# A list schedule that treats the SBUF port of VectorE and GpSimd as one resource, and an activation that stays in its PSUM bank

## The chip, the cores and the metric

The kernel runs on one core of one Trainium2 chip. The metric is the device time of one execution, in microseconds, lower is better; it is a little longer than the span from the first to the last instruction that the profiler records.

## The reference

Three layers follow each other: a linear attention with RMS norm, a block with a squared ReLU, and a block with SiLU. Matrices are float32 and are multiplied to nearly float32 accuracy.

```
# attention: 8 batches x 8 heads, 576 tokens, head size 64
kv = einsum('bhsd,bhse->bhde', k, v); out = einsum('bhsd,bhde->bhse', q, kv)
x  = out / sqrt(mean(out*out, -1) + 1e-6) * g_norm          # -> 4608 x 512
# first block: w_in 512 x 2048, w_out 2048 x 512
h = x @ w_in; r = maximum(h, 0); y = (s * (r*r) + b) @ w_out
# second block, the same sizes
h = y @ w_in2; out = (h / (1 + exp(-h))) @ w_out2
```

## The kernel before, in words

Every float32 operand of a product is split into a high part (rounded by ScalarE, `rnd`, L201) and a low part (the difference, `rest`, L204), and three matmuls (high x high, high x low, low x high) make one product. The 4608 tokens are nine blocks of 512. The weights come as 64-bit numbers and are decoded on the chip: ScalarE takes the magnitude (`mag`, L284) and the low word (`carry`, L301), VectorE the sign bit and the exponent (`sign`, L288; `top`, L293), GpSimd adds the two words (`total`, L307), then ScalarE and VectorE split the result (L201, L204).

The first block runs plainly for token blocks 0 to 6, one unit for each of the 16 slices of 128 hidden features: 12 matmuls into one of two PSUM banks `h` (`mm1`), ReLU out of the bank into an SBUF tile `g` (`first`, L722), the square (`squares`: on GpSimd in token block 0, L728, on ScalarE in the others, L726), scale and bias (`affine`, L731), the split of `g` into `gh` (L201 and L204), and 12 matmuls into four accumulators (`mm2`). There are two tiles `g`. In token block 0 the weights are being decoded while the units run; that stretch reaches from about 31 to 162 us. Attention of the later token blocks and a recoding of all weights for the next stage run beside blocks 1 to 6.

The other blocks (7 and 8 in the first layer, all but block 6 in the second) go through in pairs by a Strassen scheme with seven products instead of eight (L931 for the hidden layer, L1059 to L1061 for the output). VectorE takes sums out of PSUM (`plus`, L956; `total`, L1068); the differences of the activations (`minus`, L995) and the low parts (L204) may go to VectorE or GpSimd, the sums of results (L1093, L1110) go to GpSimd. Block 6 of the second layer is again plain and ends the program.

The order on each engine is not written by hand. `Plan` (its `run`) is a list scheduler: each operation has a key, the engines that may do it with a planned duration for each, what it needs and makes, and the buffers it takes and gives back. At every step the scheduler takes, of the engines' ready operations, the one that can begin first. It writes one in-order program for each engine; on the chip an instruction that waits holds up all behind it on its engine. `both` and `both2` give the planned durations of an operation that VectorE or GpSimd may do.

Of the kernel before, what the change touches and what calls it, by code (L numbers as in the profile page):

```python
# [12 lines left out]
ALU = mybir.AluOpType  # L13


class Plan:
# [24 lines left out]
    def run(self):  # L41
# [3 lines left out]
        dma = 0.0  # L45
# [71 lines left out]
def kernel(  # L117
# [25 lines left out]
    P = 128  # L143
# [68 lines left out]
    def dma(dst, src):  # L212
# [46 lines left out]
    def decode(layer, kind, m, c, width, sfx, key, needs=(), quarter=None, made=()):  # L259
# [63 lines left out]
        add({DVE: 0.07 + width * 0.52e-3}, key - 0.45, sign, needs=[f(1)], makes=[f(2)])  # L323
        add(dve(width), key - 0.4, top, needs=[f(2)], makes=[f(3)])
        add(act(width) if layer == 0 else {DVE: 0.07 + width * 0.52e-3}, key - 0.35, carry, needs=[f(0)], makes=[f(4)])
        add({POOL: 0.19 + width * 2.46e-3}, key - 0.25, total, needs=[f(3), f(4)], makes=[f(6)] + list(made), gives=[raw])
        w = f"w{kind}{m}"
        if layer == 0:
# [4 lines left out]
            add(dve(width), key - 0.15, lo, needs=[f(7)], makes=[full], gives=[dw])  # L333
# [87 lines left out]
    def attention_pair(bb, p, key, before=None):  # L421
# [110 lines left out]
        add({DVE: 0.2}, key + 0.5, lambda e: rest(e, st["kvl"], st["kvf"], st["kvh"]), needs=[f("kvh")], makes=[f("kvl")],  # L532
# [91 lines left out]
    g_t, h_t, a_t, xs = {}, {}, {}, {}  # L624
# [57 lines left out]
    def unit(u):  # L682
# [605 lines left out]
```

## Time and profile before

| what | value |
|---|---|
| median of 3 runs | 1610.23 us (1607.92 to 1613.66) |
| the profiled execution, its own time | 1611.14 us |
| its span, first to last instruction | 1609.4 us |
| mean granted TensorE clock | 0.996 |
| busy: PE, VectorE, ScalarE, GpSimd | 1576.7, 1072.7, 903.4, 1031.6 us |

The profile is of one execution. The busy time of PE is a union of overlapping matmuls, so a busy PE may still start fewer matmuls than it could. The busy time of VectorE and GpSimd holds the time in which an instruction has started and stands still.

### The profile page before, as it was taken

Reading aid. Unit: us, or ns where it says so; the run is one execution under the profiler, and the core shown is the slowest. Engines: PE = TensorE matmul, PEld = TensorE weight load, DVE = VectorE, ACT = ScalarE, POOL = GpSimd, SP = SyncE. Lnnn points to the kernel's source line nnn. Section 1 sums busy time; section 2 is a strip of 40 time slices with the busy share of each in tenths; the row PEclk is TensorE's granted clock in tenths of the full one; section 3 lists DMA queues with packets and bytes.
Section 4 is the critical chain, followed back from the end, with each engine's and each line's share of the span. In section 5 each row is a group of like instructions: output and inputs, shape, how many; then the busy total and the mean of one; then the engine's idle time right before and its main releaser. Section 6 shows DMA issues by size and latency. Waiting matters only on the chain.

```text
span 1609.4 us, 23497 instructions
## 1 busy us (share of the span) xinstructions
PE 1576.7 (98%) x7473; PEld 1279.5 (80%) x7473; DVE 1072.7 (67%) x1526; ACT 903.4 (56%) x1700; POOL 1031.6 (64%) x865
## 2 busy tenths in 40 slices
PE   8889999999999999999999999999999999999999
PEld 6667888878877787777888878888888888888887
DVE  5997667677677877552767876786688558856510
ACT  5787656666666766765766453544354435444222
POOL 4775777655556665565557796777678667866632
PEclk9999999999999999999999999999999999999999
DMA  9755678666667786799567786878687868776684
GB/s 222 186 165 134 219 232 249 206 189 188 189 202 220 217 243 189 235 335 314 182 193 226 250 292 187 259 222 241 192 286 197 233 196 265 196 239 193 204 212 134
DMA packets 377147, 351.30 MB, mean 218 GB/s; under 512 B 178240, under 2 KB 288832, under 8 KB 377024
## 3 DMA queue, kind: packets, MB, share of 16 engines
q1 hardware_dynamic: 376896, 349.81, 72.8%
q8 instruction: 59, 0.97, 0.3%
q14 instruction: 64, 0.52, 0.1%
q0 software_dynamic: 128, 0.00, 0.0%
HBM read 254.28 MB, written 95.42 MB: 217 GB/s over the span
## 4 chain that ended last, share of the span: by engine, by line
PE 81%; DMA 8%; DVE 6%; issue 2%; SPq 1%; ACT 1%; POOL 1%; DVEq 0%; POOLq 0%; ACTq 0%
PE hp L931 23%; PE acc L1059 8%; PE acc L1061 8%; PE acc L1060 8%; PE h L198 5%; PE h L196 5%; PE h L197 5%; PE acc L196 4%; PE acc L197 4%; PE acc L198 4%; DMA xt_d<-tmp 2%; SPq L213 1%; DVE raw L288 1%; PE kv_ps L481 1%; DVE raw L293 1%
## 5 line engine op out<-in xcount | busy, mean ns | idle before, releaser
L931 PE MATMUL hp<-xo,win 128*128 128x512 f32 x1680 | 424.4, 390 | 5.0 <-DVE tmp L956 5.0
L931 PEld LDWEIGHTS hp<-xo,win 128*128 128x128 f32 x1680 | 315.0, 188 | 74.9 <-DVE tmp L956 7.3
L204 POOL TENSOR_TENSOR g<-tmp,g 128x512 fp32r<-128x512 f32 x167 | 237.4, 1429 | 175.8 <-ACT g L201 174.8
L1068 DVE TENSOR_TENSOR ya<-acc,ya 128x512 f32<-128x512 f32 x210 | 142.8, 684 | 120.8 <-PE acc L1061 120.3
L1059 PE MATMUL acc<-g,wout 128*128 128x512 f32 x560 | 219.6, 392 | 0.1
L1061 PE MATMUL acc<-g,wout 128*128 128x512 f32 x560 | 218.9, 391 | 0.0
L1060 PE MATMUL acc<-g,wout 128*128 128x512 f32 x560 | 218.9, 391 | 0.0
L201 ACT ACTIVATE g<-tmp 128x512 fp32r<-128x512 f32 x280 | 172.7, 629 | 81.1 <-POOL tmp L995 34.5
L722 ACT ACTIVATE g<-h 128x512 f32<-128x512 f32 x128 | 76.2, 595 | 209.8 <-PE h L198 205.7
L198 PE MATMUL h<-xh,wi 128*128 128x512 f32 x448 | 177.1, 395 | 9.5 <-DVE wi L204 9.4
L196 PE MATMUL acc<-gh,wo 128*128 128x512 f32 x448 | 182.5, 407 | 1.7 <-DVE y L210 0.9
L196 PE MATMUL h<-xh,wi 128*128 128x512 f32 x448 | 177.8, 397 | 0.3 <-ACT wi L201 0.3
L197 PE MATMUL acc<-gh,wo 128*128 128x512 f32 x448 | 176.1, 393 | 1.6 <-POOL gh L204 1.6
L197 PE MATMUL h<-xl,wi 128*128 128x512 f32 x448 | 176.4, 394 | 0.3 <-POOL xl L204 0.3
L198 PE MATMUL acc<-gh,wo 128*128 128x512 f32 x448 | 175.5, 392 | 0.0
L956 DVE TENSOR_TENSOR tmp<-hp,tmp 128x512 f32<-128x512 f32 x200 | 136.7, 685 | 53.9 <-PE hp L931 50.6
L204 DVE TENSOR_TENSOR g<-tmp,g 128x512 fp32r<-128x512 f32 x113 | 150.9, 1354 | 19.5 <-ACT g L201 18.8
L995 POOL TENSOR_TENSOR tmp<-tmp 128x512 f32<-128x512 f32 x85 | 133.5, 1577 | 28.5 <-ACT tmp L977 14.0
L977 ACT ACTIVATE tmp<-tmp 128x512 f32<-128x512 f32 x120 | 75.5, 629 | 125.7 <-DVE tmp L956 125.1
L204 POOL TENSOR_TENSOR gh<-g,gh 128x512 fp32r<-128x512 f32 x70 | 97.7, 1397 | 60.6 <-ACT gh L201 50.8
L1059 PEld LDWEIGHTS acc<-g,wout 128*128 128x128 f32 x560 | 105.1, 188 | 23.4 <-DVE ya L1068 0.9
L1061 PEld LDWEIGHTS acc<-g,wout 128*128 128x128 f32 x560 | 105.2, 188 | 23.3
(142 smaller groups left out, 2963.3 us busy)
## 6 DMA issues: line engine op xcount, KB each, us to landing
wout<-wo SPq DMA_DIRECT2D x312, 256.0 KB, 3.9
win<-wi SPq DMA_DIRECT2D x120, 512.0 KB, 4.8
wi<-rq SPq DMA_DIRECT2D x192, 128.0 KB, 2.5
wo<-rq SPq DMA_DIRECT2D x192, 128.0 KB, 2.4
win<-wi SPq DMA_DIRECT2D x72, 256.0 KB, 3.9
raw<-in_moe_w_out_dram SPq DMA_DIRECT2D x38, 256.0 KB, 3.5
raw<-in_moe_w_in_dram SPq DMA_DIRECT2D x34, 256.0 KB, 3.0
xt_d<-tmp SPq DMA_DIRECT2D x32, 256.0 KB, 5.7
```

The source lines that it names most:

```text
L196: nc.tensor.matmul(ps, wh, xh, start=first, stop=False)
L197: nc.tensor.matmul(ps, wh, xl, start=False, stop=False)
L198: nc.tensor.matmul(ps, wl, xh, start=False, stop=last)
L201: nc.scalar.activation(hi, src, AF.Copy)
L204: eng[e].tensor_tensor(lo, src, f32(hi), op=ALU.subtract)
L931: nc.tensor.matmul(ps, w[:, wn, f_], x_[:, xn], start=first and n == 0, stop=kk == KH - 1 and n == 2, skip_group_check=True)
L956: nc.vector.tensor_tensor(t, bank[me, a], tmp[b_, me], op=ALU.add)
L995: eng[e].tensor_tensor(t, tmp[a, me], tmp[b_, me], op=ALU.subtract)
L1059: nc.tensor.matmul(ps, w[:, 0, dd], gh, start=a == 0, stop=False)
L1060: nc.tensor.matmul(ps, w[:, 0, dd], gl, start=False, stop=False)
L1061: nc.tensor.matmul(ps, w[:, 1, dd], gh, start=False, stop=a == 1)
L1068: nc.vector.tensor_tensor(y2[tp, i, d], st["ps"], y2[tp, i, d], op=ALU.add)
```

## The change

The scheduler gets a fifth kind of resource. A duration of the class `Port` marks an operation that uses the SBUF port which VectorE and GpSimd share; such an operation begins, in the plan, only after the last one so marked has ended, on whichever of the two engines. The planned durations of these operations become shorter (those of an instruction alone). An operation that two engines may do is no longer a candidate on an engine if the other would end it sooner (`best_on`). And in the plain units `g` is no longer a tile in SBUF: ReLU, square and affine work in place in the PSUM bank `h`, the split reads the bank, and the bank is given back only after the low part is taken. The square of token block 0 moves from GpSimd to ScalarE, the low part of all plain units goes to VectorE alone, and the two tiles `g0`, `g1` go to the pool `ya` of the Strassen sums from the start.

```diff
+class Port(float):
+    pass
...
         def begin(e, op, when):
-            t = max(free[e], when)
+            t = max(free[e], when, port if isinstance(op[2][e], Port) else 0.0)
...
+        def best_on(e, t, op, ready):
+            if len(op[2]) == 1:
+                return True
+            for e2, d2 in op[2].items():
+                if e2 != e:
+                    t2 = begin(e2, op, ready[e2][op[1]][1])
+                    if t2 is not None and (t2 + d2, e2) < (t + op[2][e], e):
+                        return False
+            return True
...
-                cand = [(t, op) for t, op in cand if t is not None]
+                cand = [(t, op) for t, op in cand if t is not None and best_on(e, t, op, ready)]
...
                 free[e] = end = t + op[2][e]
+                if isinstance(op[2][e], Port):
+                    port = end
...
-                 "g": ["g0", "g1"], "gh": ["gh0", "gh1", "gh2"], "y": ["y0", "y1"],
+                 "gh": ["gh0", "gh1", "gh2"], "y": ["y0", "y1"],
...
     def both(n):
-
-        return {DVE: 0.1 + n * 1.8e-3, POOL: 0.15 + n * 2.4e-3}
-
-    def both2(n):
-        return {DVE: 0.15 + n * 2.25e-3, POOL: 0.15 + n * 2.65e-3}
+        return {DVE: Port(0.07 + n * 1.05e-3), POOL: Port(0.15 + n * 2.36e-3)}
...
-        add({POOL: 0.19 + width * 2.46e-3}, key - 0.25, total, needs=[f(3), f(4)], makes=[f(6)] + list(made), gives=[raw])
+        add({POOL: Port(0.27 + width * 1.67e-3)}, key - 0.25, total, needs=[f(3), f(4)], makes=[f(6)] + list(made), gives=[raw])
...
-            nc.scalar.activation(g_t[u], h_t[u], AF.Relu if layer == 0 else AF.Silu)
+            nc.scalar.activation(h_t[u], h_t[u], AF.Relu if layer == 0 else AF.Silu)
...
-        add(act(T), u + 0.1, first, needs=[("mm1", u, KD - 1)], makes=[("r", u)], takes=[g], gives=[("h", u)])
+        add(act(T), u + 0.1, first, needs=[("mm1", u, KD - 1)], makes=[("r", u)])
         src = ("r", u)
         if layer == 0:
-            add({POOL: 1.1} if t == 0 else act2(T), u + 0.2, squares, needs=[src], makes=[("sq", u)])
-            add({ACT: 0.81}, u + 0.25, affine, needs=[("sq", u)], makes=[("aff", u)])
+            add(act(T), u + 0.2, squares, needs=[src], makes=[("sq", u)])
+            add({ACT: 0.73}, u + 0.25, affine, needs=[("sq", u)], makes=[("aff", u)])
...
-        add({POOL: 1.4} if layer == 0 and t == 0 else both(T), u + 0.35, g_lo, needs=[("gh", u)], makes=[("gl", u)], gives=[g])
+        add({DVE: 0.69}, u + 0.35, g_lo, needs=[("gh", u)], makes=[("gl", u)], gives=[("h", u)])
```

In the whole program GpSimd goes from 870 to 273 instructions and VectorE from 1528 to 2094. ScalarE gets 16 squares more.

GpSimd in token block 0 (`dw<-raw` is `total` of a weight, `g<-g` the square, `gh<-g,gh` the low part of a unit), before:

```order
L307 TENSOR_TENSOR dw_942<-raw_902 128x512
L204 TENSOR_TENSOR gh_976<-g_936,gh_975 128x512
L307 TENSOR_TENSOR dw_987<-raw_932 128x512
L728 TENSOR_TENSOR g_1014<-g_1014 128x512
L307 TENSOR_TENSOR dw_1008<-raw_949 128x512
L307 TENSOR_TENSOR dw_1023<-raw_978 128x512
L204 TENSOR_TENSOR gh_1058<-g_1014,gh_1057 128x512
L728 TENSOR_TENSOR g_1068<-g_1068 128x512
```

and now:

```order
L319 TENSOR_TENSOR dw_918<-raw_835 128x512
L319 TENSOR_TENSOR dw_927<-raw_863 128x512
L319 TENSOR_TENSOR dw_946<-raw_898 128x512
L319 TENSOR_TENSOR dw_1000<-raw_959 128x512
L319 TENSOR_TENSOR dw_1040<-raw_982 128x512
```

Only the sums of the weights are left on GpSimd there. VectorE at the same place, around the low parts of weights `wo6` and `wi8`, before:

```order
L204 TENSOR_TENSOR wi7_1036<-dw_987,wi7_1036 128x512
L288 TENSOR_SCALAR raw_994<-raw_994 128x512
L293 SCALAR_TENSOR_TENSOR raw_994<-dw_1042,raw_994 128x512
L578 RECIPROCAL rms_1073<-rms_1073 128x16
L583 STREAM_TRANSPOSE sq_969<-rms_1073 128x512
L204 TENSOR_TENSOR wo6_1075<-dw_1008,wo6_1075 128x512
L590 SCALAR_TENSOR_TENSOR x32_802<-o_ps_944,vecs_121,sq_969 128x512
L204 TENSOR_TENSOR wi8_1085<-dw_1023,wi8_1085 128x512
```

and now:

```order
L220 TENSOR_TENSOR gh_1029<-h_939,gh_1028 128x512
L305 SCALAR_TENSOR_TENSOR raw_959<-dw_1000,raw_959 128x512
L300 TENSOR_SCALAR raw_982<-raw_982 128x512
L220 TENSOR_TENSOR wi7_1061<-dw_946,wi7_1061 128x512
L590 RECIPROCAL rms_1071<-rms_1071 128x16
L305 SCALAR_TENSOR_TENSOR raw_982<-dw_1040,raw_982 128x512
L595 STREAM_TRANSPOSE sq_1009<-rms_1071 128x512
L220 TENSOR_TENSOR gh_1093<-h_1004,gh_1092 128x512
L220 TENSOR_TENSOR wo6_1089<-dw_1000,wo6_1089 128x512
L602 SCALAR_TENSOR_TENSOR x32_891<-o_ps_990,vecs_121,sq_1009 128x512
L220 TENSOR_TENSOR wi8_1117<-dw_1040,wi8_1117 128x512
```

The same operations stand there with one low part of a unit (`gh<-h,gh`) more per unit, read from the PSUM bank. PE before the first output matmuls of unit 0 (`h_760` is the bank of unit 3, all 24 matmuls of units 2 and 3 stand ahead of the output; `acc<-gh,wo0` is the output of unit 0), before:

```order
L196 MATMUL h_760<-xh_645,wi3_728 128x512
L197 MATMUL h_760<-xl_646,wi3_728 128x512
L198 MATMUL h_760<-xh_645,wi3_728 128x512
L508 MATMUL r_ps_792<-qT_708,kvf1_131 128x64
L196 MATMUL acc_796<-gh_757,wo0_583 128x512
L197 MATMUL acc_796<-gh_758,wo0_583 128x512
L198 MATMUL acc_796<-gh_757,wo0_583 128x512
```

and now, after 33 short filler matmuls (`warm`; `h_767` is the bank of unit 2):

```order
L1231 MATMUL warm_146<-zeros_119 128x256
L212 MATMUL acc_758<-gh_731,wo0_616 128x512
L213 MATMUL acc_758<-gh_732,wo0_616 128x512
L214 MATMUL acc_758<-gh_731,wo0_616 128x512
L212 MATMUL h_767<-xh_359,wi2_675 128x512
L213 MATMUL h_767<-xl_360,wi2_675 128x512
L214 MATMUL h_767<-xh_359,wi2_675 128x512
L212 MATMUL acc_776<-gh_731,wo0_616 128x512
```

Units 2 and 3 of the hidden layer have moved behind the first output of unit 0, whose bank unit 2 needs. VectorE in the Strassen stage, around one group of activations (`g2` are the low parts, `hp` and `acc` PSUM banks), before:

```order
L995 TENSOR_TENSOR tmp_11808<-tmp_11691,tmp_11689 128x512
L995 TENSOR_TENSOR tmp_11822<-tmp_11735,tmp_11808 128x512
L204 TENSOR_TENSOR g2_11829<-tmp_11808,g2_11828 128x512
L204 TENSOR_TENSOR g2_11841<-tmp_11822,g2_11841 128x512
L956 TENSOR_TENSOR tmp_11864<-hp_11795,tmp_11799 128x512
```

and now:

```order
L997 TENSOR_TENSOR tmp_11713<-tmp_11548,tmp_11602 128x512
L220 TENSOR_TENSOR g2_11707<-tmp_11687,g2_11707 128x512
L997 TENSOR_TENSOR tmp_11548<-tmp_11634,tmp_11548 128x512
L997 TENSOR_TENSOR tmp_11733<-tmp_11634,tmp_11713 128x512
L220 TENSOR_TENSOR g2_11726<-tmp_11713,g2_11725 128x512
L220 TENSOR_TENSOR g2_11738<-tmp_11548,g2_11738 128x512
L997 TENSOR_TENSOR tmp_11687<-tmp_11687,tmp_11733 128x512
L220 TENSOR_TENSOR g2_11745<-tmp_11733,g2_11745 128x512
L958 TENSOR_TENSOR tmp_11772<-hp_11709,tmp_11715 128x512
```

The differences and low parts that GpSimd took stand in VectorE's own queue, eight ahead of the next sum out of a PSUM bank instead of four.

## Rows read from the trace of the kernel before

**Rows 1.** Windows; columns: length, PE, PEld, DVE, ACT, POOL busy, clock, DMA, GB/s.
```profile
31.00:162.00 131.00, 118.28 (x619) 91.36 (x618) 118.04 (x160) 101.11 (x200) 90.03 (x74) 0.96 0.63 169
162.00:640.00 478.00, 473.20 (x2431) 382.98 (x2431) 342.43 (x608) 318.28 (x676) 294.60 (x328) 1.00 0.71 212
640.00:800.00 160.00, 154.09 (x670) 124.60 (x668) 80.90 (x93) 106.47 (x182) 93.45 (x71) 1.00 0.82 268
800.00:1560.00 760.00, 759.21 (x3322) 623.05 (x3321) 517.13 (x640) 351.86 (x590) 530.99 (x367) 1.00 0.75 225
```
**Rows 2.** Waits of PE, 31 to 162 us: total, times, longest.
```profile
PE h L198 <- DVE wi L204: 9.4, 7, 3.1
```
**Rows 3.** Timeline of PE: start, duration; units 0 and 16 begin here.
```profile
30.93 0.48 PE L196 MATMUL h<-xh,wi 128*128 128x512 f32 x1
...
151.06 0.40 PE L198 MATMUL h<-xh,wi 128*128 128x512 f32 x1
151.29 0.39 PE L196 MATMUL h<-xh,wi 128*128 128x512 f32 x1
```
**Rows 4.** Groups of VectorE by form, 31 to 162 us.
```profile
L293 DVE SCALAR_TENSOR_TENSOR raw<-dw,raw 128x512 uint32<-128x512 uint32 x26 | 29.1, 1121 | 0.5
L288 DVE TENSOR_SCALAR raw<-raw 128x512 uint32<-128x512 uint32 x26 | 23.8, 920 | 1.9 <-ACT dw L284 1.9
L204 DVE TENSOR_TENSOR wi<-dw,wi 128x512 fp32r<-128x512 f32 x15 | 15.7, 1045 | 0.0
L204 DVE TENSOR_TENSOR wo<-dw,wo 128x512 fp32r<-128x512 f32 x13 | 12.2, 935 | 2.3 <-ACT wo L201 2.3
```
**Rows 5.** Timeline of VectorE, 82 to 91 us.
```profile
82.30 1.26 DVE L288 TENSOR_SCALAR raw<-raw 128x512 uint32<-128x512 uint32 x1
...
90.10 0.68 DVE L293 SCALAR_TENSOR_TENSOR raw<-dw,raw 128x512 uint32<-128x512 uint32 x1
90.71 0.41 DVE L288 TENSOR_SCALAR raw<-raw 128x512 uint32<-128x512 uint32 x1
```
**Rows 6.** Timeline of GpSimd, 82 to 100 us.
```profile
82.00 1.27 POOL L307 TENSOR_TENSOR dw<-raw 128x512 uint32<-128x512 uint32 x1 [0.78 <-ACT gh L201]
...
98.72 1.04 POOL L307 TENSOR_TENSOR dw<-raw 128x512 uint32<-128x512 uint32 x1 [0.68 <-ACT raw L301]
```
**Rows 7.** Groups of GpSimd by form, 31 to 162 us.
```profile
L307 POOL TENSOR_TENSOR dw<-raw 128x512 uint32<-128x512 uint32 x27 | 33.8, 1252 | 22.1 <-ACT dw L284 5.2 <-DVE raw L293 4.3 <-ACT raw L301 3.3
L204 POOL TENSOR_TENSOR gh<-g,gh 128x512 fp32r<-128x512 f32 x16 | 24.6, 1546 | 4.5 <-ACT gh L201 4.5
```
**Rows 8.** Tile g, 36 to 53 us: ns least, median, most; first to last start.
```profile
L722 ACT ACTIVATE g<-h x3: 584/597/601, 43.9 to 52.6; 128x512 f32<-128x512 f32 x3
L731 ACT ACTIVATE g<-g,vecs x2: 799/800/800, 48.4 to 49.9; 128x512 f32<-128x512 f32 x2
L201 ACT ACTIVATE gh<-g x2: 616/617/618, 49.3 to 50.7; 128x512 fp32r<-128x512 f32 x2
L204 POOL TENSOR_TENSOR gh<-g,gh x2: 1717/1732/1746, 50.9 to 52.6; 128x512 fp32r<-128x512 f32 x2
```
**Rows 9.** Timeline of PE, 56 to 57.3 us: first output matmul of unit 0.
```profile
56.88 0.77 PE L196 MATMUL acc<-gh,wo 128*128 128x512 f32 x1
```
**Rows 10.** Waits of PE, 640 to 1560 us.
```profile
PE hp L931 <- DVE tmp L956: 5.0, 4, 2.7
```
**Rows 11.** Groups of VectorE by form, 800 to 1560 us.
```profile
L204 DVE TENSOR_TENSOR g<-tmp,g 128x512 fp32r<-128x512 f32 x106 | 140.4, 1344 | 18.6 <-ACT g L201 17.9
L956 DVE TENSOR_TENSOR tmp<-hp,tmp 128x512 f32<-128x512 f32 x184 | 125.8, 685 | 41.1 <-PE hp L931 39.9
L995 DVE TENSOR_TENSOR tmp<-tmp 128x512 f32<-128x512 f32 x69 | 77.3, 1125 | 12.9 <-POOL tmp L995 8.3 <-ACT tmp L977 2.7 <-ACT tmp L983 1.1
```
**Rows 12.** Groups of GpSimd by form, 800 to 1560 us.
```profile
L204 POOL TENSOR_TENSOR g<-tmp,g 128x512 fp32r<-128x512 f32 x155 | 219.7, 1424 | 161.2 <-ACT g L201 160.2 <-POOL tmp L995 0.9
L1093 POOL TENSOR_TENSOR ya<-ya 128x512 f32<-128x512 f32 x70 | 99.3, 1449 | 12.7 <-DVE ya L1068 12.5
```

More of the change, by code (lines that the diff above doesn't have):

```diff
@@ L44, in run @@
         free["PE"] = self.PE_START
-        dma = 0.0
+        dma = port = 0.0
         known, waiting, left = {}, {}, {}
@@ L322, in decode @@
             makes=[f(1)], takes=[dw])
-        add({DVE: 0.07 + width * 0.52e-3}, key - 0.45, sign, needs=[f(1)], makes=[f(2)])
-        add(dve(width), key - 0.4, top, needs=[f(2)], makes=[f(3)])
-        add(act(width) if layer == 0 else {DVE: 0.07 + width * 0.52e-3}, key - 0.35, carry, needs=[f(0)], makes=[f(4)])
-        add({POOL: 0.19 + width * 2.46e-3}, key - 0.25, total, needs=[f(3), f(4)], makes=[f(6)] + list(made), gives=[raw])
+        add({DVE: Port(0.07 + width * 0.62e-3)}, key - 0.45, sign, needs=[f(1)], makes=[f(2)])
+        add({DVE: both(width)[DVE]}, key - 0.4, top, needs=[f(2)], makes=[f(3)])
+        add(act(width) if layer == 0 else {DVE: Port(0.07 + width * 0.62e-3)}, key - 0.35, carry, needs=[f(0)], makes=[f(4)])
+        add({POOL: Port(0.27 + width * 1.67e-3)}, key - 0.25, total, needs=[f(3), f(4)], makes=[f(6)] + list(made), gives=[raw])
         w = f"w{kind}{m}"
@@ L332, in decode @@
                 takes=takes)
-            add(dve(width), key - 0.15, lo, needs=[f(7)], makes=[full], gives=[dw])
+            add({DVE: both(width)[DVE]}, key - 0.15, lo, needs=[f(7)], makes=[full], gives=[dw])
     def rq(b):
@@ L531, in attention_pair @@
         add({ACT: 0.2}, key + 0.4, kv_hi, needs=[f("kvf")], makes=[f("kvh")], takes=[b["kvs"]], gives=[b["kvf"]])
-        add({DVE: 0.2}, key + 0.5, lambda e: rest(e, st["kvl"], st["kvf"], st["kvh"]), needs=[f("kvh")], makes=[f("kvl")],
+        add({DVE: Port(0.2)}, key + 0.5, lambda e: rest(e, st["kvl"], st["kvf"], st["kvh"]), needs=[f("kvh")], makes=[f("kvl")],
             gives=[b["kvf"]])
@@ L897, in pair_x @@
         add(act2(T), k2, hi, needs=[("xl2",) + me], makes=[("pxh",) + me], takes=[b_], gives=[rb])
-        add(both2(T), k2 + 0.02, lo, needs=[("pxh",) + me], makes=[("xo", i, tp, kk)], gives=[rb])
+        add(both(T), k2 + 0.02, lo, needs=[("pxh",) + me], makes=[("xo", i, tp, kk)], gives=[rb])
     def win_loads(tp, j):
@@ L999, in hidden @@
         kt = k(6) + 0.2
[L1000 to L1003 removed]
+        add(both(T), kt, minus("e", "a", "d"), needs=sg("a", "d"), makes=sg("e"), takes=[tb["e"]])
+        add(both(T), kt + 0.02, minus("f", "b", "e"), needs=sg("b", "e"), makes=sg("f"), takes=[tb["f"]])
+        add(both(T), kt + 0.01, minus("a", "b", "a"), needs=sg("b", "e"), makes=sg("a2"))
+        add(both(T), kt + 0.1, minus("c", "c", "f"), needs=sg("f") + [("gl",) + me + (B21,)], makes=sg("c2"))
         for i, src, ready, kk, gives in (
@@ L1018, in hidden @@
             add(act2(T), kk, hi, needs=ready, makes=[("gh",) + me + (i,)], takes=[gb])
-            add(both2(T), kk + 0.03, lo, needs=[("gh",) + me + (i,)], makes=[("gl",) + me + (i,)],
+            add(both(T), kk + 0.03, lo, needs=[("gh",) + me + (i,)], makes=[("gl",) + me + (i,)],
                 gives={B11: [], B22: [], B21: [], T1: [tb["e"]], T3: [tb["a"]], T2: [], T4: [tb["c"]]}[i])
@@ L1093, in go @@
                     eng[e].tensor_tensor(y2[tp, i, d], y2[tp, i, d], y2[tp, j, d], op=ALU.add)
-                add({POOL: 1.3}, key + 0.02 * n, go, needs=needs + ([o(0)] if n == 1 else []), makes=[o(n)], gives=[y(x) for x in gives])
+                add({POOL: Port(1.36)}, key + 0.02 * n, go, needs=needs + ([o(0)] if n == 1 else []), makes=[o(n)], gives=[y(x) for x in gives])
             parts = ((0, 0, B21, 1), (0, 1, B22, 4), (1, 1, T1, 5), (1, 0, T4, 6))
@@ L1110, in go @@
                         eng[e].tensor_tensor(y2[tp, dst, d], y2[tp, a, d], y2[tp, b_, d], op=ALU.subtract)
-                    add({POOL: 1.3}, key + 0.3 + 0.02 * m, go, needs=needs, makes=[("xs0", tp, so, d)])
+                    add({POOL: Port(1.36)}, key + 0.3 + 0.02 * m, go, needs=needs, makes=[("xs0", tp, so, d)])
                     after = {T1: [("xs0", tp, T2, d)], T2: [("xs0", tp, T4, d)]}.get(so, [])
```

26 lines of the change are left out of this document (6 added, 20 removed).

## The prediction

> **What bounds the kernel now.** I read the busy times by stretch first. From 162 to 640 us PE is busy for 473.2 of 478 us, from 800 to 1560 us for 759.2 of 760 [rows 1]. There PE is the bound, the change takes no matmul of the product away, and nothing is to be won. What can be won lies in two stretches: token block 0 with the decoding of the weights (31 to 162 us, PE busy 118.3 of 131) and the passage into the Strassen stage (640 to 800 us, 154.1 of 160) [rows 1].
>
> In the first of them the waits of PE name one cause, the low part of a decoded weight from VectorE, 9.4 us of visible idleness [rows 2]. The visible idleness is not all of the loss. Matmuls that follow each other start 0.23 us apart [rows 3], so the 24 matmuls of a unit need 24 x 0.23 = 5.5 us; unit 0 begins at 30.93 and unit 16 at 151.29 us [rows 3], which is 7.5 us per unit. Sixteen units lose 32 us, of which the attention matmuls that share the stretch take a part. The granted clock has a mean of 0.96 there, against 1.00 in the stretches that PE fills [rows 1].
>
> VectorE is busy for 118.0 of these 131 us, ScalarE for 101.1, GpSimd for 90.0 [rows 1]. But VectorE does not work all that time. The sign of a half weight takes 0.41 us alone and 0.92 in the mean; `top` 0.68 alone and 1.12 in the mean; the low parts, with two SBUF inputs of the same size, 1.05 and 0.94 [rows 4, 5]. The slow ones lie over GpSimd's instructions: the sign that starts at 82.30 takes 1.26 us beside a sum that runs from 82.00 to 83.27 [rows 5, 6]. So VectorE stands behind GpSimd, and PE behind VectorE.
>
> **The lock, part by part.** The lost time of VectorE in the stretch is 26 x (0.92 - 0.41) + 26 x (1.12 - 0.68) + 15 x (1.045 - 0.68) + 13 x (0.935 - 0.68) = 13.3 + 11.4 + 5.5 + 3.3 = 33.5 us [rows 4, 5]. What holds it up are GpSimd's 90 us [rows 1]. The squares and the low parts of the units leave GpSimd, as do three `xl` and one `qTl`; what stays are 27 sums of 1.04 us alone, 28 us [rows 6, 7], and, in the order of instructions, eight half as wide, at half of that 4 us (an estimate). That is 32 of 90. If the loss goes with GpSimd's time, 33.5 x 32/90 = 12 us are left and 21.5 saved.
>
> VectorE also gets work: 16 low parts read from PSUM and about four instructions of the same size. Alone and back to back they start about 0.61 us apart [rows 5]: 20 x 0.61 = 12 us. A VectorE difference with a PSUM input is no dearer than 0.685 us in the Strassen stage [rows 11], the price of one alone. Net VectorE has 118 - 21.5 + 12 = 108.5 us to do; at the same filling (118 of 131) the stretch takes 120.5 us: **-10 us**. Bounds: if the remaining 32 us of GpSimd all stand in VectorE's way, VectorE has 118 - 1.5 + 12 = 128.5 us, the stretch is 12 us longer; if none do, 118 - 33.5 + 12 = 96.5, 24 us shorter.
>
> The Trainium skill, page "SBUF — State Buffer", section "SBUF: two separate sides", says that the shared port is an exclusive lock, not a split of bandwidth: the engine that starts first keeps it for the whole instruction and the other blocks. The trace agrees with the blocking (1.26 against 0.41 us). By that rule each of the 35 remaining sums can hold up one VectorE instruction for half its length in the mean, an estimate of 27 x 0.52 + 8 x 0.26 = 16 us left in place of 12, and the saving in this stretch would be about 6 us in place of 10. I take the share of busy time, since it needs no guess at who starts first.
>
> **The squares on ScalarE and the bank in place.** Sixteen squares at about 0.62 us (a rounding of the same size [rows 8]) add 10 us; ScalarE then has 111 us. No row shows ScalarE writing into PSUM. The nearest are a pass out of PSUM at 0.597 and the affine at 0.800 [rows 8]; with 0.60 for all, the affine would lose 16 x 0.2 = 3 us, with 0.80 for square and ReLU the sum would gain 6. I take no change, since reading PSUM, the half of the step that is shown, is a little cheaper than reading SBUF. ScalarE's 111 us lie beside VectorE's 108.5 in a stretch of 120, so they cost nothing in the sum; they limit the gain: no more than 131 - 111 = 20 us.
>
> The Trainium skill, page "ScalarE: Activation LUTs", section "Step-by-step: what each stage is for", calls PSUM the faster destination for ScalarE; no run here shows it yet, and by it the lower end would hold.
>
> **The first output.** Units 2 and 3 now stand behind unit 0's first output, because their banks are given back late. In the trace unit 0 goes from its ReLU at 43.9 us to the end of its low part at 50.9 + 1.7 = 52.6 [rows 8], and the first output matmul starts at 56.88 [rows 9]. Without GpSimd the chain is 0.60 + 0.62 + 0.80 + 0.62 + 0.68 = 3.3 us, and three other ScalarE instructions between at about 0.6 make it 5.1: ready at 49.0. Then the 24 matmuls that moved behind it, 5.5 us, so that the same work is done at 54.5 in place of 56.9: **-2 us**. Bounds: if the chain is no shorter (52.6), 5.5 are added to 52.6, 58.1, +1; with fillers and a weight `wo0` that comes late, +4; at best -4.
>
> **Passage into the Strassen stage.** PE waits 5.0 us there for sums out of PSUM on VectorE, four times [rows 10]. Those are behind differences and low parts that lose to the lock. I take two fifths of it: **-2 us**, between 0 and -5 (+3 if the transfers between the stages, which do not change, meet later ones of the decoding).
>
> **The Strassen stage.** VectorE loses 106 x (1.344 - 0.68) + 69 x (1.125 - 0.68) = 101 us to the lock there [rows 5, 11]. GpSimd keeps the sums of results, 99.3 of 531 us [rows 1, 12] and a little more, so some 80 of these go. What GpSimd gives up is (531 - 99)/1.42 = some 300 instructions, 155 of them low parts [rows 1, 12]; on VectorE they take 0.61 us each, 183 us. Its load becomes 517 - 80 + 183 = 620 of 760 us. PE stays the bound; **0 us**, as long as VectorE's one queue does not make it wait. The end of the program is plain again with VectorE nearly empty: 0.
>
> **Sum.** -10 - 2 - 2 + 0 = -14 us from 1611.1, the profiled execution's own time: 1597. That execution lies 0.9 us above the median of the runs shown; against the median the forecast is 1597 as well, rounded, 0.8% faster. What a measurement of this kernel can tell from no change is about 0.3%, 5 us: under 1605.4 is faster, over 1615.1 slower.
>
> **Rivals.**
> - A, as above, 1588 to 1604, chance 0.60.
> - B, the bank replaces the lock (no change). A unit takes one of two banks from its first matmul to the end of its low part. Two banks give a period of half that hold. With 5.5 us of matmuls and a chain of 9.5 us the period is 7.5, that of now. The chain of unit 0 took 8.7 us before [rows 8], with two GpSimd steps in it; ScalarE's queue is fuller now (111 us in 120). Against it: the sum of its steps is 3.3 us. Gains 0 to 4 us: 1607 to 1611. Chance 0.17.
> - C, slower: VectorE's one queue in the Strassen stage. Eight differences and low parts now stand ahead of the next sum out of a bank, 8 x 0.61 = 4.9 us in place of four. A low part whose ScalarE half is late stops them all, and GpSimd no longer takes any. There are 40 such groups (five pairs of eight). At 0.35 us of PE wait for each, 14 us, the gain is gone; at 0.8 us the time is 1597 + 32 = 1629. For it: 17.9 us of VectorE's idleness there already ended with a rounding on ScalarE and 39.9 with a PSUM bank [rows 11]. Against it: 620 of 760 us leaves it time. Chance 0.11, centre 1620.
> - D, the lock goes entirely and ScalarE sets the pace: -20 in block 0, -2, -4 in the passage: 1585. Chance 0.12.
>
> B also stands for the case that the order in the plan changes little on the chip, since the plan has no say in who gets the port.
>
> The likeliest is A, 1597. The range 1585 to 1612 takes in A, B and most of D, and leaves out C. Faster 0.72 (A and D), same 0.17, slower 0.11.
>
> **What would show it.** In the profile of the changed kernel: token block 0's units begin about 6.6 to 6.9 us apart; `sign` and `top` there have means near 0.6 and 0.85; GpSimd is busy for some 35 us in the stretch and ScalarE for over 90% of it; PE's wait for the low part of `wi` is smaller, and a wait for `gh` from VectorE, if B is right, stands in its place. From 800 to 1560 us PE is full, with VectorE near 620 us. If C is right, PE has waits for VectorE at L958 or L1070 all along this stretch. The prediction is wrong if ScalarE's passes into PSUM cost 0.8 us or more, if the low parts from PSUM are held up by GpSimd after all, or if the decoding is bound by its four raw buffers and the loads into them rather than by VectorE.

## The result

The changed kernel takes 1626.54 us (median of 4 runs, 1625.23 to 1627.40), the kernel before 1611.30 (4 runs, 1607.92 to 1613.66). The ratio is 1.0095, with a 95% interval of 1.0075 to 1.0116: slower by about 15 us. The profiled execution of the changed kernel took 1625.96 us, its span 1623.9 us.

The busy times by stretch, of the changed kernel (columns as in [rows 1]):

```profile
31.00:162.00 131.00, 126.53 (x711) 101.56 (x710) 104.79 (x198) 113.21 (x233) 39.02 (x39) 0.97 0.69 188
162.00:640.00 478.00, 476.05 (x2431) 386.51 (x2431) 340.46 (x824) 318.00 (x696) 91.28 (x121) 1.00 0.73 217
640.00:800.00 160.00, 155.19 (x668) 125.69 (x667) 93.18 (x146) 100.86 (x168) 0.00 (x0) 0.99 0.77 255
800.00:1560.00 760.00, 740.04 (x3197) 603.01 (x3196) 599.58 (x881) 343.68 (x578) 138.22 (x94) 0.99 0.72 217
```

Against [rows 1], PE does 92 matmuls more in the first stretch (711 against 619), and 125 fewer in the last (3197 against 3322). At 0.227 us for each the last stretch alone loses 28 us.

Where the program stands at three places says the same. The timeline of PE in the changed kernel, at the first output matmul of unit 16, at the first matmul of the Strassen stage (L933) and at the first one of the last plain block:

```profile
155.67 0.39 PE L212 MATMUL acc<-gh,wo 128*128 128x512 f32 x1
...
723.16 0.39 PE L933 MATMUL hp<-xo,win 128*128 128x512 f32 x1
...
1511.76 0.39 PE L212 MATMUL h<-xo,win 128*128 128x512 f32 x1
```

And the same three places in the kernel before:

```profile
164.89 0.49 PE L196 MATMUL acc<-gh,wo 128*128 128x512 f32 x1
...
738.81 0.39 PE L931 MATMUL hp<-xo,win 128*128 128x512 f32 x1
...
1497.40 0.39 PE L196 MATMUL h<-xo,win 128*128 128x512 f32 x1
```

The changed kernel is 9 us ahead at unit 16 and 16 us ahead at the Strassen stage. From there to the last block it takes 788.6 us in place of 758.6, and this length, called the stage below, is what the experiments are read by. The forecast gain came; 30 us were lost behind it.

The waits of PE in the changed kernel from 640 to 1560 us, against the one row of [rows 10]:

```profile
PE hp L933 <- DVE tmp L958: 13.1, 13, 3.6
PE hp L933 <- DMA win<-wi: 8.7, 3, 4.0
```

The second is new: PE waits for weights (`win`).

How it comes to that is seen at each change of pairs, when the sums of results of one pair (L1095) are made while the next pair runs. The timelines of GpSimd, VectorE, SP's queue and PE in the changed kernel, one such change:

```profile
1223.09 17.82 POOL L1095 TENSOR_TENSOR ya<-ya 128x512 f32<-128x512 f32 x12 [3.35 <-DMA wout<-wo]
```
```profile
1226.95 3.47 DVE L220 TENSOR_TENSOR g<-tmp,g 128x512 fp32r<-128x512 f32 x2
1230.34 0.68 DVE L1070 TENSOR_TENSOR ya<-acc,ya 128x512 f32<-128x512 f32 x1
...
1232.74 0.67 DVE L997 TENSOR_TENSOR tmp<-tmp 128x512 f32<-128x512 f32 x1
...
1234.65 3.41 DVE L997 TENSOR_TENSOR tmp<-tmp 128x512 f32<-128x512 f32 x2
1237.98 3.48 DVE L220 TENSOR_TENSOR g<-tmp,g 128x512 fp32r<-128x512 f32 x2
1241.38 0.68 DVE L997 TENSOR_TENSOR tmp<-tmp 128x512 f32<-128x512 f32 x1
...
1247.95 0.69 DVE L1125 STREAM_TRANSPOSE ya<-ya 128x512 f32<-128x512 f32 x1
```
```profile
1246.90 6.40 SPq L229 DMA_DIRECT2D out_dram<-ya  x8
1253.40 0.93 SPq L229 DMA_DIRECT2D wout<-wo  x2
1254.42 8.08 SPq L229 DMA_DIRECT2D out_dram<-ya  x12
1262.60 0.93 SPq L229 DMA_DIRECT2D wout<-wo  x2
1263.57 1.38 SPq L229 DMA_DIRECT2D win<-wi  x3
```
```profile
1245.70 3.70 PE L933 MATMUL hp<-xo,win 128*128 128x512 f32 x15 [0.89 <-DVE tmp L958]
...
1263.68 1.55 PE L933 MATMUL hp<-xo,win 128*128 128x512 f32 x6
1269.20 1.62 PE L933 MATMUL hp<-xo,win 128*128 128x512 f32 x3 [3.98 <-DMA win<-wi]
1273.18 2.41 PE L933 MATMUL hp<-xo,win 128*128 128x512 f32 x6
```

GpSimd makes twelve sums back to back, until 1240.91. Meanwhile six of VectorE's seven low parts and differences, which have two SBUF inputs, take 1.7 us each (the seventh, at 1232.74, takes 0.67); the moment GpSimd is done, the next takes 0.68. The sum with a PSUM input (L1070) in the middle is not held up. In this stretch VectorE is full, though in the mean of 800 to 1560 us it is not (the window, columns as in [rows 1]):

```profile
1223.00:1250.00 27.00, 26.11 (x115) 21.22 (x114) 25.67 (x33) 11.57 (x21) 17.82 (x12) 1.00 0.70 183
```

So VectorE is late, first with the sums that PE waits for (0.89 us at 1245.70), then with the transposes of results (L1125). It does not wait for GpSimd's sums themselves: its waits from 800 to 1512 us name only PE and ScalarE. SP issues in order: the first stores of these results wait for the transposes, the rest come out in lumps of 8 and 12, and the loads of the next weights stand behind them until 1263.57. PE waits 3.98 us for them, and runs slowly after that: six matmuls take 2.41 us at 1273.18, and 1.55 at 1263.68. The windows show the granted clock (the column ahead of the last two), 0.75 in the mean of the ten microseconds, between the levels of 1.2 and 2.4 GHz:

```profile
1260.00:1270.00 10.00, 6.02 (x25) 4.66 (x24) 3.37 (x5) 4.55 (x8) 0.00 (x0) 0.91 0.80 201
1270.00:1280.00 10.00, 10.00 (x34) 7.97 (x34) 5.10 (x8) 3.38 (x6) 0.00 (x0) 0.75 0.83 295
1280.00:1300.00 20.00, 20.00 (x89) 16.41 (x88) 14.90 (x25) 7.52 (x12) 0.00 (x0) 1.00 0.56 174
```

PE does 34 matmuls from 1270 to 1280 and 44.5 in ten later ones: a full column of busy time, and 2.4 us lost in it.

The groups of VectorE and GpSimd in the changed kernel, 800 to 1560 us, answer to [rows 11, 12]:

```profile
L220 DVE TENSOR_TENSOR g<-tmp,g 128x512 fp32r<-128x512 f32 x254 | 190.0, 763 | 31.8 <-ACT g L217 31.7
...
L958 DVE TENSOR_TENSOR tmp<-hp,tmp 128x512 f32<-128x512 f32 x180 | 123.2, 686 | 35.9 <-PE hp L933 34.8
L997 DVE TENSOR_TENSOR tmp<-tmp 128x512 f32<-128x512 f32 x144 | 114.0, 812 | 3.5 <-ACT tmp L979 2.8
```
```profile
L1095 POOL TENSOR_TENSOR ya<-ya 128x512 f32<-128x512 f32 x70 | 102.3, 1497 | 153.3 <-DVE ya L1070 149.9 <-DMA wout<-wo 3.4
```

The lock takes 254 x (0.763 - 0.68) + 144 x (0.812 - 0.68) = 40 us of VectorE now, against 101 in the kernel before. It takes less and costs more: some 30 of the 40 us lie beside GpSimd's sums, at 31 operations close together, and nobody takes work off VectorE there.

### The profile page after: what moved, and what is told of

The parts are those of the page before. It is cut to its first block, busy times and chain, and to the rows that moved or that the text cites. A ratio compares the mean times of both kernels' runs of the same rounds, so it can differ in the third digit from the quotient of the medians.

```text
span 1623.9 us, 23268 instructions
## 1 busy us (share of the span) xinstructions
PE 1585.1 (98%) x7500; PEld 1286.6 (79%) x7500; DVE 1162.4 (72%) x2092; ACT 904.4 (56%) x1731; POOL 273.3 (17%) x268
## 4 chain that ended last, share of the span: by engine, by line
PE 76%; DVE 11%; DMA 7%; SPq 3%; ACT 2%; issue 1%; POOL 0%; DVEq 0%; ACTq 0%; POOLq 0%
PE hp L933 19%; PE acc L1061 6%; PE acc L1062 6%; PE acc L1063 6%; PE h L212 6%; PE h L213 6%; PE h L214 6%; PE acc L212 5%; PE acc L213 5%; PE acc L214 5%; SPq L229 3%; DVE g L220 3%; DVE tmp L997 2%; DMA win<-wi 1%; DVE xo L220 1%
## 5 line engine op out<-in xcount | busy, mean ns | idle before, releaser
L933 PE MATMUL hp<-xo,win 128*128 128x512 f32 x1680 | 432.7, 394 | 21.8 <-DVE tmp L958 13.1
L933 PEld LDWEIGHTS hp<-xo,win 128*128 128x128 f32 x1680 | 317.5, 190 | 97.4 <-DVE tmp L958 19.2
L220 DVE TENSOR_TENSOR g<-tmp,g 128x512 fp32r<-128x512 f32 x280 | 207.2, 756 | 33.1 <-ACT g L217 33.0
L727 ACT ACTIVATE h<-h 128x512 f32<-128x512 f32 x128 | 74.6, 583 | 210.8 <-PE h L214 210.4
L1070 DVE TENSOR_TENSOR ya<-acc,ya 128x512 f32<-128x512 f32 x210 | 142.7, 686 | 51.7 <-PE acc L1063 49.4
L958 DVE TENSOR_TENSOR tmp<-hp,tmp 128x512 f32<-128x512 f32 x200 | 136.8, 686 | 45.4 <-PE hp L933 44.3
L1095 POOL TENSOR_TENSOR ya<-ya 128x512 f32<-128x512 f32 x70 | 102.3, 1497 | 153.3 <-DVE ya L1070 149.9
L997 DVE TENSOR_TENSOR tmp<-tmp 128x512 f32<-128x512 f32 x160 | 124.7, 800 | 3.6 <-ACT tmp L979 2.8
L1062 PEld LDWEIGHTS acc<-g,wout 128*128 128x128 f32 x560 | 105.8, 189 | 24.3 <-DVE g L220 1.6
L1061 PEld LDWEIGHTS acc<-g,wout 128*128 128x128 f32 x560 | 105.7, 189 | 24.4 <-ACT g L217 1.7
L1063 PEld LDWEIGHTS acc<-g,wout 128*128 128x128 f32 x560 | 105.9, 189 | 23.5
```

The source lines that it names most:

```text
L220: eng[e].tensor_tensor(lo, src, f32(hi), op=ALU.subtract)
L933: nc.tensor.matmul(ps, w[:, wn, f_], x_[:, xn], start=first and n == 0, stop=kk == KH - 1 and n == 2, skip_group_check=True)
L958: nc.vector.tensor_tensor(t, bank[me, a], tmp[b_, me], op=ALU.add)
L997: eng[e].tensor_tensor(t, tmp[a, me], tmp[b_, me], op=ALU.subtract)
L1061: nc.tensor.matmul(ps, w[:, 0, dd], gh, start=a == 0, stop=False)
L1062: nc.tensor.matmul(ps, w[:, 0, dd], gl, start=False, stop=False)
```

## The experiments

The theory at the start: the 30 us are the lock between the sums of results on GpSimd and VectorE, which now carries all low parts and differences alone. Its rivals: VectorE has too much to do, whoever holds the port (rival C in its general form); or the plan's order is at fault. Times of each run stand beside the kernel before on the same chip, as a ratio with its 95% interval.

**One half of the change: the bank without the port.** In the kernel before, ReLU, square and affine work in place in the bank, as in the changed kernel; the scheduler is the old one.

```diff
-            nc.scalar.activation(g_t[u], h_t[u], AF.Relu if layer == 0 else AF.Silu)
+            nc.scalar.activation(h_t[u], h_t[u], AF.Relu if layer == 0 else AF.Silu)
...
-        add({POOL: 1.4} if layer == 0 and t == 0 else both(T), u + 0.35, g_lo, needs=[("gh", u)], makes=[("gl", u)], gives=[g])
+        add({DVE: 0.69}, u + 0.35, g_lo, needs=[("gh", u)], makes=[("gl", u)], gives=[("h", u)])
```

> The kernel before with one part of the change alone: g stays in its PSUM bank (square on ScalarE, low part on VectorE); planned durations, engine choice and the Strassen stage are as before. If the gain up to the Strassen stage (first output of the last plain unit 16 us earlier) comes from taking squares and low parts off GpSimd, this kernel keeps most of it, 8 to 14 us, and loses nothing later: 1598 to 1604 us. If it comes from the plan with the port, about 1611 us.

Measured: 1611.07 us, 0.9987 (0.9974 to 0.9999). At unit 16 it is 4 us ahead of the kernel before, and no more later. In token block 0 GpSimd is still busy for 54.8 us, with five low parts of q and four of x on it. Two groups of VectorE in block 0:

```profile
L293 DVE SCALAR_TENSOR_TENSOR raw<-dw,raw 128x512 uint32<-128x512 uint32 x26 | 22.1, 852 | 0.6
L288 DVE TENSOR_SCALAR raw<-raw 128x512 uint32<-128x512 uint32 x26 | 17.9, 692 | 1.6 <-ACT dw L284 1.6
```

The lock takes less than in [rows 4] (1121 and 920 ns), but it is not gone. The expectation was too high: the bank is less than half of the gain of block 0.

**The other half: the port without the bank.** `g` lies in SBUF again, with square and low part of block 0 on GpSimd, marked as users of the port.

```diff
-            add(act(T), u + 0.2, squares, needs=[src], makes=[("sq", u)])
+            add({POOL: Port(1.1)} if t == 0 else act2(T), u + 0.2, squares, needs=[src], makes=[("sq", u)])
...
-        add({DVE: 0.69}, u + 0.35, g_lo, needs=[("gh", u)], makes=[("gl", u)], gives=[("h", u)])
+        add({POOL: Port(1.36)} if layer == 0 and t == 0 else both(T), u + 0.35, g_lo, needs=[("gh", u)], makes=[("gl", u)], gives=[g])
```

> The other part alone: the port as a resource, free durations and the engine choice, with g in SBUF as before. If the loss lies in the Strassen stage and comes from the engine choice, it is all here, about 30 us, and the gain of token block 0 is small (0 to 6 us): 1630 to 1641 us. If the loss needs the bank, about 1605 us.

Measured: 1655.92 us, 1.0260 (1.0232 to 1.0287), above both forecasts. Block 0 loses 18 us (unit 16 at 182.8 us): the plan keeps VectorE and GpSimd off each other, and may have more work for one port than it holds, which was not tested further. The stage takes 799 us, 40 more than before, and PE's waits are those of the changed kernel, only larger (16.0 us for L968, 9.8 for the weights). So the loss in the stage belongs to the scheduler's half (port, durations and engine choice, which were not tried one by one), and the gain of block 0 needs both halves.

**The Strassen stage as before.** The changed kernel, with the old durations, not marked, for what both engines may do in the Strassen stage.

```diff
-            if len(op[2]) == 1:
+            if len(op[2]) == 1 or not isinstance(op[2].get("POOL"), Port):
...
-            add(both(T), kk + 0.03, lo, needs=[("gh",) + me + (i,)], makes=[("gl",) + me + (i,)],
+            add(both2(T), kk + 0.03, lo, needs=[("gh",) + me + (i,)], makes=[("gl",) + me + (i,)],
...
-                add({POOL: Port(1.36)}, key + 0.02 * n, go, needs=needs + ([o(0)] if n == 1 else []), makes=[o(n)], gives=[y(x) for x in gives])
+                add({POOL: 1.3}, key + 0.02 * n, go, needs=needs + ([o(0)] if n == 1 else []), makes=[o(n)], gives=[y(x) for x in gives])
```

> The changed kernel with the planned durations and the free choice of engine of before in the Strassen stage alone (differences, low parts and input splits may go to GpSimd again, no port there). If handing these to VectorE costs the 30 us, the time is 1611 - 16 = 1595 us, between 1592 and 1600. If the loss comes from something else that the change brought (the tiles g0 and g1 given to the sums, the earlier arrival at the passage), 1615 us or more.

Measured: 1593.60 us, 0.9873 (0.9851 to 0.9896), faster than both kernels. The stage takes 757.3 us. Its window, two groups of VectorE and one of GpSimd:

```profile
800.00:1560.00 760.00, 758.38 (x3319) 622.41 (x3318) 512.97 (x638) 343.52 (x577) 510.39 (x352) 1.00 0.76 225
```
```profile
L220 DVE TENSOR_TENSOR g<-tmp,g 128x512 fp32r<-128x512 f32 x104 | 139.7, 1363 | 18.1 <-ACT g L217 17.5
...
L1000 DVE TENSOR_TENSOR tmp<-tmp 128x512 f32<-128x512 f32 x65 | 71.2, 1100 | 12.6 <-POOL tmp L1000 8.8 <-ACT tmp L982 2.1 <-ACT tmp L988 1.1
```
```profile
L220 POOL TENSOR_TENSOR g<-tmp,g 128x512 fp32r<-128x512 f32 x150 | 211.8, 1419 | 159.0 <-ACT g L217 156.6 <-POOL tmp L1000 1.6 <-DMA win<-wi 0.8
```

VectorE's operations are as slow as ever here (1363 ns), and PE is full: the lock costs PE nothing here, where more than half of the low parts (150 of 254) lie on the other engine.

**The sums of results made narrow.** The changed kernel, with an eighth of each sum.

```diff
-                    eng[e].tensor_tensor(y2[tp, i, d], y2[tp, i, d], y2[tp, j, d], op=ALU.add)
+                    eng[e].tensor_tensor(y2[tp, i, d][:, :64], y2[tp, i, d][:, :64], y2[tp, j, d][:, :64], op=ALU.add)
```

> The changed kernel in which GpSimd adds only 64 of 512 columns of each result sum (this part of the output is left out). GpSimd then holds the port for some 0.3 us in place of 1.3 at each of 70 sums, and all else stands as it was. Lock theory (VectorE, which now does everything else, alternates with the sums of results at each change of pairs, falls behind, and output stores and weight loads queue behind it): the waits of PE at the changes of pairs go, 1596 to 1604 us. Queue theory (VectorE's one queue is too full or stops at late ScalarE results, whatever GpSimd does): 1618 us or more.

Measured: 1603.70 us, 0.9941 (0.9918 to 0.9963). The stage takes 765.0 us. The order on the engines is the same, only GpSimd's time is taken away (70 sums take 26.3 us in place of 102.3), and 24 of the 30 us go. The wait for the weights goes too, though nothing about SP was changed; this row is left:

```profile
PE hp L933 <- DVE tmp L958: 7.5, 10, 1.9
```

Narrow sums are also done sooner, but that is no rival: VectorE waited for none of them in the stage of the changed kernel. The profiled execution (1600.59 us) is the fastest of five; by the medians of this chip 10 us stay against the kernel with the Strassen stage as before (1603.70 and 1593.60), by the stages 8 (765.0 and 757.3).

**Sums of results on either engine.** The changed kernel, with one more choice for the plan at L1095 (and at L1112).

```diff
-                add({POOL: Port(1.36)}, key + 0.02 * n, go, needs=needs + ([o(0)] if n == 1 else []), makes=[o(n)], gives=[y(x) for x in gives])
+                add(both(T), key + 0.02 * n, go, needs=needs + ([o(0)] if n == 1 else []), makes=[o(n)], gives=[y(x) for x in gives])
```

> The changed kernel, but the sums of results of the Strassen stage (L1095, L1112) may go to VectorE or GpSimd like the other sums; the plan then leaves some 16 of them on GpSimd. Lock theory (VectorE's operations with two SBUF inputs take about 1.7 us in place of 0.6 while GpSimd does result sums back to back, and everything behind them on VectorE comes late): some 65 sums at about 0.6 us, 40 us, are added to VectorE's 600 of 760 us from 800 to 1560, but the slow operations at the changes of pairs go; the Strassen stage, 788.6 us in the changed kernel and 758.6 before, comes out between 762 and 775, the time between 1600 and 1612. Load theory (VectorE's one queue has too much work, whoever holds the port): its load grows from 72% to some 75% less what the lock took; the time stays at 1622 or more.

Measured: 1622.50 us, 1.0069 (1.0045 to 1.0093), and a stage of 780.2 us: the number that the load theory gave. But the trace shows another cause beside load. The timelines of SP's queue and of PE at a change of pairs:

```profile
1081.47 15.36 SPq L229 DMA_DIRECT2D out_dram<-ya  x28
...
1097.96 0.38 SPq L229 DMA_DIRECT2D win<-wi  x1
```
```profile
1102.71 0.93 PE L933 MATMUL hp<-xo,win 128*128 128x512 f32 x3 [3.44 <-DMA win<-wi]
```

VectorE makes eight transposes almost in a row, so 28 stores come due together, at 0.55 us each; the plan put them ahead of the weights. PE's wait for L958 went down to 7.1 us, that for the weights up to 11.1. In two of its three waits for weights the granted clock falls behind the wait (0.62 in the mean from 1262 to 1266 us, 0.51 from 1424 to 1429); behind the one shown it stays at 1.00 (1103 to 1110), so the half clock that the next expectation puts there is a misreading. Two more runs were made to tell this from load.

**Stores with a later key, in that kernel and in the changed one.** Loads of weights that can be issued at the same time then go first; 28 stores in a row become pieces of 4 and 8, and in the changed kernel two more weight loads stand ahead of the last 12 stores.

```diff
-                add({"SP": 1.92 if BLOCKS[tp][n] < NB - 1 else 3.84}, key + 0.3, store, needs=[("yz", tp, c, n, d)],
+                add({"SP": 1.92 if BLOCKS[tp][n] < NB - 1 else 3.84}, key + 30, store, needs=[("yz", tp, c, n, d)],
```

> The kernel in which the sums of results may go to VectorE, but the output stores get a later key, so that loads of weights that are ready go first in SP's order: 28 stores in a row become pieces of 4 and 8 with weight loads between. Theory (queue of SP: 28 stores issued one after the other take 15.4 us, at 1081.47 us for one, the weights of the next pair stand behind them, and PE waits 3.4 us at 1102.71 and then runs at half the clock): PE's wait for win from wi, 11.1 us in all, goes nearly, the Strassen stage falls from 780.2 us to 762 to 768, the time from 1622 to 1603 to 1611. Rival (VectorE's load of 75% is what costs, and the order of SP matters little): 1617 to 1625.

> The changed kernel with the same later key for the output stores; the plan puts two more weight loads ahead of the last 12 stores of a pair. If the queue of SP is the way in which late transposes cost time, PE's wait for win from wi (8.7 us) goes and the time falls by 6 to 14 us, to 1612 to 1620. If the sums that PE waits for are late by the lock alone, PE's wait for L958 (13.1 us) stays or grows and the time stays at 1622 to 1630.

Measured: with the sums on either engine 1607.98 us, 0.9965 (0.9949 to 0.9980), stage 769.7; in the changed kernel 1613.72 us, 0.9999 (0.9985 to 1.0013), stage 774.5. Neither has a wait for the weights any more. In the changed kernel the other wait stays as it was, as the row of its waits shows:

```profile
PE hp L933 <- DVE tmp L958: 13.0, 13, 3.6
```

So, with the changed kernel's order, 14 us of the 30 came by way of SP's queue. For the kernel with sums on either engine the load theory falls as the whole account: one key, no work less, takes the time from 1622.50 to 1607.98 us and the stage from 780.2 to 769.7. It does not fall for the rest: 769.7 is over the 762 to 768 that was forecast and 11 us over the stage of before, PE still waits 10.1 us for L958, and nothing here tells VectorE's load from another cause of these 11.

**Both repairs together.** The narrow sums and the later key.

> Both single repairs of the changed kernel in one: the sums of results add 64 of 512 columns only (the rest of those outputs is left out), and the output stores have the later key. One theory: the two shares are the whole loss; the Strassen stage, 788.6 us in the changed kernel, 774.3 with the later stores alone and some 765 with the narrow sums alone, comes down to 757 to 762, near the 758.6 of before, and the time to 1593 to 1601. Rival: VectorE's load without GpSimd's help costs something of its own, whatever the lock and SP's order do; the stage stays at 764 or more and the time at 1602 or more.

Measured: 1605.38 us, 0.9960 (0.9946 to 0.9973), stage 764.3 us, as with the narrow sums alone. The two repairs don't add up: without the lock at the sums the transposes come early enough for the weights, and SP's order doesn't matter. What is left, 764.3 against 758.6, fits the rival: 6 us with VectorE's one queue, while PE's waits for L958 are 7.2 us in all, against 5.0 [rows 10]. That it is load alone is not shown: GpSimd still splits inputs in this stage, and some 8 us of VectorE's time are lost to the lock beside those splits.

**The stores on GpSimd's queue.**

```diff
-                            dma(out[t_ * S:t_ * S + T, cols].rearrange("(b r) d -> r b d", r=Q), src.rearrange("p (b d) -> p b d", d=Q))
+                            nc.gpsimd.dma_start(out=out[t_ * S:t_ * S + T, cols].rearrange("(b r) d -> r b d", r=Q), in_=src.rearrange("p (b d) -> p b d", d=Q))
```

> The changed kernel, but the output stores of the Strassen results are issued by GpSimd and not by SP. SP issues in order: in the changed kernel it waits 24.1 us for VectorE's transposes of results (L1125), ten times, with loads of the next pair's weights behind them, and PE waits 8.7 us for such loads. Theory 1 (a good part of the 30 us lost in the Strassen stage comes by this queue: late transposes, late stores, late weights, and a lower granted clock behind PE's wait): the wait for the weights goes, and the time falls by 8 to 14 us, to 1612 to 1619. Theory 2 (the sums that PE waits for, L958, are late by the lock itself and the queue of SP adds little): the time stays at 1623 to 1630.

Measured: 1641.63 us, 1.0187 (1.0162 to 1.0213), stage 801.4 us: neither theory. The wait for the weights is gone as theory 1 said, but PE's wait for L958 is 33.9 us. The stores hold up GpSimd's sums, so that seven of them come due together, and then, in GpSimd's timeline and VectorE's:

```profile
1243.55 2.57 POOL L1133 DMA_DIRECT2D out_dram<-ya  x4 [1.48 <-DVE ya L1125]
1246.13 8.62 POOL L1095 TENSOR_TENSOR ya<-ya 128x512 f32<-128x512 f32 x7
```
```profile
1245.56 9.74 DVE L997 TENSOR_TENSOR tmp<-tmp 128x512 f32<-128x512 f32 x1
1255.23 0.68 DVE L220 TENSOR_TENSOR g<-tmp,g 128x512 fp32r<-128x512 f32 x1
```

One difference stands still through all seven. That happens in three of the changes of pairs, at 9.7 us each. As a test of SP's queue this run is worth nothing, since it moved the sums; the runs with the later key took its place.

**The sums not marked in the plan.** The changed kernel; the sums' planned duration stays 1.36 us.

```diff
-                add({POOL: Port(1.36)}, key + 0.02 * n, go, needs=needs + ([o(0)] if n == 1 else []), makes=[o(n)], gives=[y(x) for x in gives])
+                add({POOL: 1.36}, key + 0.02 * n, go, needs=needs + ([o(0)] if n == 1 else []), makes=[o(n)], gives=[y(x) for x in gives])
```

> The changed kernel, but the sums of results are not marked as users of the port in the plan (their planned duration on GpSimd stays 1.36 us); all else that VectorE and GpSimd may both do still is. If the chip's lock between GpSimd's sums and VectorE's operations causes the loss, whatever the plan says of it, the time stays within 5 us of that of the changed kernel, 1621 to 1631. If the plan's order causes it (operations held back in the plan because the port is taken, so that they stand late in the queue), the time falls by 10 us or more, under 1617.

Measured: 1631.32 us, 1.0128 (1.0099 to 1.0157), stage 795.3 us. The mark is no cause of the loss; if anything it is worth some 5 us (the two intervals overlap). But the loss takes another way here. PE waits for no weights from 720 to 1560 us, and for the sums twice as long as in the changed kernel:

```profile
PE hp L933 <- DVE tmp L958: 27.9, 12, 5.9
```

Three of these waits, one at each of three changes of pairs, take 5.9 us; most low parts and differences beside GpSimd's sums take 1.7 us, as in the changed kernel. So how much of the loss goes through SP's queue and how much through late sums depends on the order.

## Why the prediction was wrong

**Block 0, -10, and the first output, -2.** Right in kind, too large together: 9 us at unit 16 in place of 12. That 9 comes so near to 12 is in part luck. Unit 4 starts at 58.87 us against 64.01, so 5 of the 9 us are there right behind the first outputs, for which -2 was put down (and -4 at best); from there to unit 16 it is 4, where the lock was to give 10. The signs that were named: units start 7.0 us apart (from 30.09 to 142.52 us, sixteen of them), not 6.6 to 6.9. The lock went further than forecast; the rows of VectorE in block 0 of the changed kernel answer to [rows 4]:

```profile
L305 DVE SCALAR_TENSOR_TENSOR raw<-dw,raw 128x512 uint32<-128x512 uint32 x27 | 19.4, 728 | 0.0
...
L300 DVE TENSOR_SCALAR raw<-raw 128x512 uint32<-128x512 uint32 x26 | 10.6, 419 | 0.1
```

`top` takes 0.73 us and `sign` 0.42, where 0.85 and 0.6 were named; VectorE is busy for 104.8 us, not 108.5. PE's wait for `wi` is gone, and no wait for `gh` took its place, so rival B falls. ScalarE is busy for 113 us of 131, 86% and not over 90%. The step that failed in this term is "at the same filling (118 of 131)": VectorE had less to do than forecast and still the stretch did not shrink with it, since VectorE no longer set the pace. It is busy for 80% now, and PE has stretches in which it is full, as from 65 to 100 us:

```profile
65.00:100.00 35.00, 35.00 (x183) 28.56 (x183) 28.91 (x51) 32.78 (x63) 13.12 (x12) 1.00 0.75 193
```

What else kept the gain back was not tried. The passes of ScalarE in the bank were taken at no change; they turned out cheaper (groups of ScalarE in block 0, against 800, 597 and about 620 ns in [rows 8]):

```profile
L733 ACT ACTIVATE h<-h,vecs 128x512 f32<-128x512 f32 x19 | 14.2, 749 | 0.1
L730 ACT ACTIVATE h<-h 128x512 f32<-128x512 f32 x19 | 11.2, 592 | 0.1
L727 ACT ACTIVATE h<-h 128x512 f32<-128x512 f32 x19 | 11.2, 590 | 6.0 <-PE h L214 5.7
```

The rule of the Trainium skill that the prediction named (page "ScalarE: Activation LUTs", section "Step-by-step: what each stage is for": PSUM is ScalarE's faster destination) is borne out only faintly: in ReLU, the one pass whose source stayed the same, 590 ns stand against 597; in the other two the source moved into PSUM as well, and their gain can't be put down to the destination.

**The passage, -2.** Right in size: PE's waits for these sums from 640 to 800 us are 2.0 us in the changed kernel and 4.3 before (of the 5.0 of [rows 10]). But from unit 16 to the Strassen stage the changed kernel gains 6 us, and most of it before the passage: it is 9 us ahead at unit 16 and 13 at unit 96 (634.02 against 647.39 us), in the plain blocks where "nothing is to be won" (PE busy for 476.05 of 478 us there, against 473.20). The run with the bank alone gains nothing there (it is 4 us ahead at both ends), so this comes with the scheduler's part.

**The Strassen stage, 0.** This is the step that failed. "Its load becomes 517 - 80 + 183 = 620 of 760 us. PE stays the bound; 0 us, as long as VectorE's one queue does not make it wait." The load was right, 600 of 760. The conclusion from it was not: it is a mean over 760 us, and the loss falls into the some 20 us at each change of pairs in which GpSimd makes the sums of results. VectorE's operations with two SBUF inputs go at 1.7 us there, and it has all of them now; from 1223 to 1250 us it is busy for 25.67 of 27. That GpSimd keeps these sums stood in the prediction, as a subtraction from a total.

Rival C had the sign, and VectorE's queue; the range left it out on "620 of 760 us leaves it time". Its mechanism, late halves from ScalarE in 40 groups, is not what the runs show; that 1626.54 us lies between its 1620 and 1629 is luck. Of the 30 us, 24 go when GpSimd's time at the sums goes; 14 of them reach PE through SP's queue, as late weights and a lower clock, which no rival named. Some 6 us by the stages, up to 10 by the medians, stay without the lock at the sums, and are the most that was real of C.

The sum by what was measured: -9 in block 0, -6 up to the Strassen stage, +30 in it, +15 in all; the span grew by 14.5 us.

## What to carry to other kernels

A load that is under 100% in the mean says little where one engine's work comes in bursts: look at the stretch in which the other engine is solid, and count what the first must do in it. An engine that a lock slows down can still be worth its share of the work: with work on both engines PE stayed full although VectorE's operations took twice their time. And where an in-order queue carried both results out and weights in, late results made late weights; a later key for the stores gave back half of the loss.

## What was not expected of the hardware

Where GpSimd's sums and VectorE's operations meet, neither order is given by the plan. With twelve sums in a row a waiting operation of VectorE got in after about one sum (1.7 us a piece, a little less than a sum of 8.62 / 7 = 1.23 and a difference of 0.6 together); with seven in a row that followed on DMA issues of GpSimd, one VectorE operation stood for 9.74 us, and got the port only after the last. The Trainium skill (page "SBUF — State Buffer", section "SBUF: two separate sides") says that the engine that starts first holds the port for its whole instruction. The changed kernel agrees: the difference at 1232.74 starts 0.06 us ahead of a sum and takes 0.67 us, and that sum takes 1.77. The other trace does not, by the start times: the difference that stood starts at 1245.56, during the last DMA issue and 0.57 us ahead of the first sum. Who gets the port next differs too, and why was not settled.

VectorE's transposes, which have one SBUF input, and its sums with one input from PSUM were not held up beside the same sums: 0.70 and 0.68 us. One SBUF input is no safe sign, though: `sign` has only one, and took 1.26 us beside a sum [rows 5, 6].
